# One weight DMA fewer and one zero product fewer in the tail of a decode kernel

## The chip, the core and the metric

The kernel runs on one core of one Trainium2 chip. The metric is the device time of one execution in microseconds (us). Each kernel was run several times; the medians are quoted together with the single runs where less than one per cent matters. All runs quoted here were classed "fast": none fell into the slower state that some executions show. A profile of one execution of each kernel gives the busy times, the waits and the timeline. Times inside a profile count from the start of its span, which is about 1.5 us shorter than the device time (660.1 against 661.56 us for the kernel before).

Engines are named as in the profile: PE is the engine of the matrix products, PEld its weight loads, DVE the vector engine, ACT the scalar engine, POOL the GpSimd engine, SP the sync engine, which issues nearly all DMAs here. A DMA "lands" when the last part of its data has come and its semaphore, for which the engines wait, has its full count.

## The reference, cut to what matters

One decode step of a transformer block for a batch of 4: attention over a cache of 4096 positions and 32 heads, then a dense layer with the Mish activation.

```python
x = A_x                                                    # (4, 1, 640), bf16
h = x + _A_ref(_layernorm(x), k_cache, v_cache, wq, wo)    # caches (4, 32, 4096, 128)
h2 = h + _B_ref(_layernorm(h), w1, b1, w2)                 # w1 (640, 1728), w2 (1728, 640)
# _A_ref: q = x @ wq; softmax(q k^T / sqrt(128)) v; then @ wo, wo (4096, 640)
# _B_ref: act = mish(x @ w1 + b1); act @ w2
```

Nearly all of the work is moving data: the two caches alone are 268 MB of the 283 MB that the kernel reads.

## The kernel before

SP issues the loads in the order of use: K and V tiles, then `wo`, `w1`, the last 64 rows of `w2` (`w2_tail`), and `w2` in four pieces of 5, 4, 3 and 1 row blocks. `wo` comes in four groups; the last group is cut into pieces of 4, 3 and 1 of its 8 rows per partition, so that PE can start on the first rows before the last have come.

```python
FR = (5, 4, 3, 1)                                   # w2's pieces, in blocks of 128 rows
FS = [sum(FR[:k]) for k in range(len(FR) + 1)]      # 0, 5, 9, 12, 13
WOS = [(k, 0, G) for k in range(NHG - 1)] + [(NHG - 1, a, b) for a, b in ((0, 4), (4, 7), (7, G))]
...
# SP
for n, (q, j0, j1) in enumerate(WOS):
    load(sp, wo_sb[:, q, j0:j1, :], A_wo[...][:, j0:j1, :], ("wo", q, j0), f"W{n}")
# then w1 in three pieces, w2_tail, w2 in the four pieces of FR; each has its own semaphore
```

On PE the tail is: products with `wo`; the layer norm's sums; products with `w1` into `h1`; then DVE and ACT compute Mish; then products with `w2`. Between them stand "zero products", which multiply zeros into a bank of PSUM (the memory that PE writes to) that nobody reads. They keep PE active while it waits.

```python
def busy(n):                                        # n products of 128 x 512 zeros
    for k in range(n):
        (mm_same if k else mm)(
            o_full[:, :], ident[:, :], zeros[:, :].to_broadcast([P, 512]), True, True
        )
...
pe.need("act")
def w2_mm(j): ...                                   # two products of 128 x 320, for the halves of the output
pe.need("w2t")
w2_mm(FM)
for j0, j1 in zip(FS, FS[1:]):
    if j0 == FS[2]:
        busy(3)                                     # ahead of w2's third piece
    pe.need(("w2", j0))                             # wait for this piece's DMA
    for j in range(j0, j1):
        w2_mm(j)
```

After the last product DVE and ACT copy the two halves of the output (`o_bf`), and SP and ACT store them.

The softmax here doesn't subtract the row's maximum and nothing guards it: scores larger than these inputs give would overflow.

Of the kernel before, what the change touches and what calls it, by code (L numbers as in the profile page):

```python
# [78 lines left out]
def kernel(  # L79
# [20 lines left out]
    G = 8  # L100
# [5 lines left out]
    NHG = H // G  # L106
# [135 lines left out]
    x_rows = A_x.rearrange("b s d -> (b s) d")  # L242
    out_rows = out.rearrange("b s d -> (b s) d")

    WOS = [(k, 0, G) for k in range(NHG - 1)] + [(NHG - 1, a, b) for a, b in ((0, 4), (4, 7), (7, G))]
    W1S = (0, 2, DC - 1, DC)

    KS = {0: "A", 1: "B", 2: "A", 3: "B"}
# [12 lines left out]
    def load(p, dst, src, key, sem):  # L261
        p.do(lambda: p.eng.dma_start(out=dst, in_=src), key, sem, 16)  # L262
# [43 lines left out]
    def sync_prog():  # L306
# [19 lines left out]
        sp.need(("F", NT - 1, NS - 1))  # L326
        for n, (q, j0, j1) in enumerate(WOS):
            load(
# [5 lines left out]
        for k, (c0, c1) in enumerate(zip(W1S, W1S[1:])):  # L334
            load(sp, w1_sb[:, c0:c1, :], w1_v[:, c0:c1, :], ("w1", c0), f"W{len(WOS) + k}")
        load(sp, w2_tail[0:FT, :], B_w2[FM * P : F, :], "w2t", "WT")
        sp.need(("PV", NT - 2))
        for k, (j0, j1) in enumerate(zip(FS, FS[1:])):
            load(
                sp, w2_sb[:, j0:j1, :],  # L340
                B_w2[j0 * P : j1 * P, :].rearrange("(p j) n -> p j n", j=j1 - j0), ("w2", j0),
                f"W{len(WOS) + len(W1S) - 1 + k}",
            )
# [376 lines left out]
    def mm(out_, lhsT, rhs, start, stop, mark=None, skip=True):  # L720
        pe.do(
            lambda: nc.tensor.matmul(  # L722
                out_, lhsT=lhsT, rhs=rhs, start=start, stop=stop, skip_group_check=skip
            ),
            mark, "PE",
        )
# [18 lines left out]
    def runs(cols, j):  # L745
        k, i = FG[j]
        cols = cols[:, FS[k] * P : FS[k + 1] * P].rearrange("p (f i) -> p i f", i=FR[k])
        return cols[:, i, :]
# [71 lines left out]
    def o_mm(i):  # L820
        b = i % N
        pe.need(("pvc", i))
        for r in range(RQ):
            mm(
                o_ps, selo[:, r, BG - G - b * G : 2 * BG - G - b * G], pv_sb[:, r, :],
                b == 0 and r == 0, b == N - 1 and r == RQ - 1, ("O", i) if r == RQ - 1 else None,
            )

    def l_mm(hg):
        pe.need(("rsm", hg))  # L830
        mm(l_ps, rsm[:, :, :].rearrange("p b g -> p (b g)"), ones[:, :], True, True, ("L", hg))

    def a_mm(hg):
        pe.need(("om", hg))
        w = om[:, :, :].rearrange("p g (q j) -> p j (g q)", j=G)
        for j in range(G):
            mm(
                a_ps[:, j, :], w[:, j, :], delta[:, :], True, True,
                ("A", hg) if j == G - 1 else None,
            )  # L840
# [25 lines left out]
    def pe_tail():  # L866
        def wo_mm(k):
            pe.need(("a", k))
            for j in range(G):
                if (k, j) in [w[:2] for w in WOS]:  # L870
                    pe.need(("wo", k, j))
                for c in range(DC):
                    w = wo_sb[:, k, j, :].rearrange("p (m c) -> p c m", c=DC)[:, c, :]
                    done = k == NHG - 1 and j == G - 1 and c == DC - 1
                    mm(
                        y_w[:, c, :, :], w, a_t[:, k, j, :].unsqueeze(1).to_broadcast([P, WD, N]),
                        False, done, "y" if done else None,
                    )

        def busy(n):  # L880
# [5 lines that stand above are left out]
        hg = NHG - 1  # L886
        pe.freeze()
        wo_mm(0)
        o_mm(NT - 1)
        l_mm(hg)  # L890
        wo_mm(1)
        a_mm(hg)
        pe.need("zeros", ("e", NT - 1, NS - 1))
        for k, w in enumerate((OC, OC, 512, 512)):
            (mm_same if k else mm)(
                red[:, k, 0:w], ident[:, :], zeros[:, :].to_broadcast([P, w]), True, False
            )
        wo_mm(2)
        wo_mm(3)
        busy(1)  # L900
        pe.need("ysum")
        mm(m_ps, ones_d[:, :], ysum[:, :], True, True, "mean")
        pe.need("sq")
        mm(sq_ps, ones_d[:, :], sq[:, :, :].rearrange("p c n -> p (c n)"), True, True, "sqm")
        busy(3)
        pe.need("cen")
        for c0, c1 in zip(W1S, W1S[1:]):
            if c1 == DC:
                pe.need("b1_lo")
                for n, part in enumerate((b1_hi, b1_lo)):  # L910
                    for j0, j1 in ((0, FC // 2 + 1), (FC // 2 + 1, FC)):
                        (mm_same if n or j0 else mm)(
                            h1_ps[:, j0:j1, :], ident[:, :], part[:, j0:j1, :], False, False
                        )
            pe.need(("w1", c0))
            for j in [FM] + list(range(FM)):
                for c in range(c0, c1):
                    w = runs(w1_sb[:, c, :], j) if j < FM else w1_sb[:, c, FM * P : F]
                    done = c == DC - 1 and j == FM - 1
                    mm(  # L920
                        h1_w[0 : (P if j < FM else FT), j, :, :], w,
                        cen[:, c, :].unsqueeze(1).to_broadcast([P, WD, N]), False, done,
                        "h1_ps" if done else None,
                    )
        pe.need("st", "ident_f")
        for c in range(DC):
            for k in range(KO):
                mm(
                    y2_ps[k * QD : k * QD + N, k, :].rearrange("b (m c) -> b c m", c=DC)[:, c, :],
                    st[:, c, :], ident_f[:, k * P // KO : (k + 1) * P // KO], False, False,  # L930
                )
        busy(4)
        pe.need("act")

        def w2_mm(j):
            rows = P if j < FM else FT
            for k in range(KO):
                cs = slice(k * OC, (k + 1) * OC)
                mm(
                    y2_ps[k * QD : k * QD + N, k, :], act[0:rows, j, :],  # L940
                    w2_sb[:, j, cs] if j < FM else w2_tail[0:FT, cs], False, j == FM - 1,
                    ("y2", k) if j == FM - 1 else None,
                )

        pe.need("w2t")
        w2_mm(FM)
        for j0, j1 in zip(FS, FS[1:]):
            if j0 == FS[2]:
                busy(3)
            pe.need(("w2", j0))  # L950
            for j in range(j0, j1):
                w2_mm(j)

    def pe_prog(live):
        pe.live = live
        pe_setup()
        pe.need("selo", "xT", "b1T")
        logs = []
        for hg in range(NHG):
            pe.log = []  # L960
            if live and hg == 0:
                with nc.tensor.Fori(0, NHG) as _:
                    pe_body(0)
                pe.live = False
            else:
                pe_body(hg)
            logs.append(pe.log)
        assert all(x == logs[0] for x in logs), logs
        pe.live = live
        pe_tail()  # L970
# [59 lines left out]
```

## Time and profile before

| | before |
|---|---|
| time, six runs | 661.54, 661.55, 661.62, 661.85, 661.87, 661.99 us; median 661.74 (the prediction had three of them, median 661.62) |
| profiled span | 660.1 us |
| mean rate of DMA over the span | 429 GB/s |
| `w1`'s second piece has landed | 651.13 us |
| `act` is computed | 655.05 us |
| `w2`'s third piece, its last row have landed | 657.2, 657.6 us |
| output copy on DVE starts | 658.21 us |

These six runs lie on two levels, about 661.6 and 661.9.

The page shows what bounds the kernel. These are the granted clock of PE, the busy share of the DMA engines (in tenths) and the rate, in 40 equal slices of the span.

```profile
PEclk9999787879659796869668678977965879786869
DMA  9999999999999999999999999999999999999997
GB/s 417 409 445 445 438 441 417 422 445 438 434 437 425 429 445 433 437 437 425 429 445 433 437 437 425 429 445 433 433 445 425 425 445 433 433 445 425 413 419 308
```

The DMA engines are full in all slices but the last. Only the last few microseconds can be a matter of anything else. The end of the chain of waits (start, length, what; it follows the last instruction back to what released it) reads:

```profile
651.13 0.04 issue
651.18 1.28 PE red L722 x29
...
654.83 0.23 DVE act L711
655.05 0.04 issue
655.10 1.68 PE red L722 x20
656.78 0.32 PE o_ps L722
657.10 0.43 PE o_ps L732 x2
657.54 0.69 PE red L722 x8
658.22 0.47 DVE o_bf L718
```

The `o_ps` entries are the zero products. They stand on the chain itself, which is odd for work that has no result. The timeline of PE, its weight loads and the copy shows how (start, length, engine, line, operation, what is written and read, count; in brackets the idle time of the engine before it, and what the profile believes ended it):

```profile
656.07 0.36 PEld L722 LDWEIGHTS red<-slotA,act 128*4 128x4 bf16 x8 [0.25 <-DMA slotA<-in_B_w_dram]
656.71 0.10 PEld L722 LDWEIGHTS o_ps<-zeros,ident 128*128 128x128 bf16 x1 [0.28 <-issue]
656.71 0.39 PE L722 MATMUL o_ps<-zeros,ident 128*128 128x512 bf16 x1
656.94 0.60 PE L732 MATMUL o_ps<-zeros,ident 128*128 128x512 bf16 x2
657.47 0.36 PEld L722 LDWEIGHTS red<-slotA,act 128*4 128x4 bf16 x8 [0.66 <-DMA slotA<-in_B_w_dram]
657.47 0.71 PE L722 MATMUL red<-slotA,act 128*4 128x320 bf16 x8
658.21 0.48 DVE L718 CAST o_bf<-red 4x320 bf16<-4x320 f32 x1 [3.17 <-PE red L722]
```

The line at 657.47 is the third piece (six loads) together with the last row (two). The bracket blames a DMA. To test that, take the issue of the two DMAs from the timeline of SP, and their time to landing from the DMA view:

```profile
640.92 1.25 SPq L262 DMA_DIRECT2D slotA<-in_B_w_dram  x1
642.21 0.97 SPq L262 DMA_DIRECT2D slotA<-in_B_w_dram  x1
...
slotA<-in_B_w_dram SPq DMA_DIRECT2D x1, 480.0 KB, 16.3
slotA<-in_B_w_dram SPq DMA_DIRECT2D x1, 160.0 KB, 15.4
```

The third piece landed at 640.92 + 16.3 = 657.2 us, the last row at 642.21 + 15.4 = 657.6 us. The semaphore events in the trace give 657.18 and 657.57 us. So the third piece lay there for 0.29 us before its first weights were loaded. What held it was the third zero product, which started at 657.16. The second piece, at 656.07, did wait for its data: it started 0.04 us after its landing (656.03).

### The profile page before, as it was taken

The page shows a single profiled execution, that of the slowest core. Times are in us where ns is not written, and L with a number is a line of the kernel's source. Part 1 is how long each engine was busy: PE and PEld are TensorE (multiplying, and loading weights), DVE is VectorE, ACT ScalarE, POOL GpSimd, SP SyncE. Part 2 cuts the span into 40 slices and gives each one's busy share as a digit, 9 for nine tenths or more (in the row PEclk, how much of TensorE's full clock was granted, in tenths as well). Part 3 has the DMA queues.
Part 4 walks back from the last instruction along what each step waited for, and adds up shares of the span by engine and source line. Part 5 has one row for each costly group of instructions (what it writes and reads, how often), then busy time and mean ns, then how long its engine had stood idle before and what let it go on. Part 6 is the DMA issues. An engine that isn't in the chain of part 4 may idle for free. (4 is left out here: it accounts for less than half of the span.)

```text
span 660.1 us, 4898 instructions
## 1 busy us (share of the span) xinstructions
PE 391.0 (59%) x2604; PEld 68.8 (10%) x1631; DVE 407.8 (62%) x255; ACT 41.1 (6%) x158; POOL 1.8 (0%) x13
## 2 busy tenths in 40 slices
PE   1365758456327595838307485828534757675878
PEld 0100100101101010101100010100110001010145
DVE  1078988295048778677219688848306798867612
ACT  0200000000000000000000000000000000000011
POOL 0000000000000000000000000000000000000000
PEclk9999787879659796869668678977965879786869
DMA  9999999999999999999999999999999999999997
GB/s 417 409 445 445 438 441 417 422 445 438 434 437 425 429 445 433 437 437 425 429 445 433 437 437 425 429 445 433 433 445 425 425 445 433 433 445 425 413 419 308
DMA packets 6883, 283.48 MB, mean 429 GB/s; under 512 B 781, under 2 KB 1113, under 8 KB 2138
## 3 DMA queue, kind: packets, MB, share of 16 engines
q1 hardware_dynamic: 6856, 283.35, 99.4%
q8 instruction: 6, 0.10, 0.1%
q14 instruction: 3, 0.02, 0.0%
q10 hardware_dynamic: 18, 0.01, 0.0%
HBM read 283.35 MB, written 0.01 MB: 429 GB/s over the span
## 5 line engine op out<-in xcount | busy, mean ns | idle before, releaser
L529 DVE TENSOR_TENSOR slotA<-slotA,q_bc 128x8192 bf16<-128x8192 bf16 x32 | 140.6, 4415 | 90.5 <-DMA slotA<-in_A_k_cache_dram 90.5
L529 DVE TENSOR_TENSOR slotB<-slotB,q_bc 128x8192 bf16<-128x8192 bf16 x32 | 140.7, 4416 | 16.5 <-DMA slotB<-in_A_k_cache_dram 16.5
L540 DVE TENSOR_REDUCE s_f<-red 128x64 f32<-128x1024 f32 x64 | 78.0, 1218 | 98.5 <-PE red L732 98.4
L732 PE MATMUL red<-slotA,ident 128*128 128x512 bf16 x480 | 137.5, 450 | 0.0
L732 PE MATMUL red<-slotB,ident 128*128 128x512 bf16 x480 | 127.3, 425 | 0.0
L722 PE MATMUL red<-slotA,ident 128*128 128x512 bf16 x32 | 14.2, 445 | 126.4 <-PEq L49 126.4
L722 PE MATMUL pv<-slotC,e 128*32 128x512 bf16 x768 | 53.1, 437 | 36.8 <-PEq L49 33.9
L722 PE MATMUL red<-slotB,ident 128*128 128x512 bf16 x32 | 14.1, 441 | 87.2 <-PEq L49 87.2
L402 ACT ACTIVATE ex<-s_f 128x64 bf16<-128x64 f32 x64 | 16.4, 256 | 512.0 <-DVE s_f L540 512.0
L554 DVE TENSOR_TENSOR e<-ex,hmask 128x512 bf16<-128x512 bf16 x64 | 39.8, 682 | 0.0
L722 PEld LDWEIGHTS pv<-slotC,e 128*32 128x32 bf16 x768 | 22.6, 108 | 95.7 <-issue 82.1
L722 PEld LDWEIGHTS red<-slotA,ident 128*128 128x128 bf16 x32 | 3.2, 99 | 195.1 <-issue 195.0
L722 PEld LDWEIGHTS red<-slotB,ident 128*128 128x128 bf16 x32 | 3.1, 98 | 169.2 <-issue 169.2
L722 PEld LDWEIGHTS o_ps<-pv_sb,selo 128*32 128x32 f32 x136 | 13.5, 109 | 65.1 <-issue 65.1
L722 PE MATMUL o_ps<-pv_sb,selo 128*32 128x128 f32 x136 | 18.0, 276 | 0.0
L722 PE MATMUL pv<-slotA,e 128*32 128x512 bf16 x256 | 14.5, 380 | 0.2 <-PEq L49 0.2
L412 ACT COPY pv_sb<-pv 128x512 f32<-128x512 f32 x16 | 9.4, 585 | 69.8 <-PE pv L722 69.8
L402 ACT ACTIVATION_READ_ACCUMULATOR ex<-s_f 128x1 f32 x64 | 11.9, 186 | 0.0
L722 PEld LDWEIGHTS pv<-slotA,e 128*32 128x32 bf16 x256 | 6.7, 97 | 23.4 <-issue 17.5
L519 DVE CAST b1T<-pv 128x13 bf16<-128x13 f32 x1 | 0.2, 173 | 14.0 <-PE pv L722 14.0
L579 DVE RECIPROCAL rl<-misc 32x1 f32<-32x1 f32 x4 | 0.6, 150 | 12.8 <-PE misc L722 12.8
L722 PE MATMUL red<-slotC,lnT 128*32 128x512 bf16 x40 | 4.5, 631 | 5.6 <-PEq L49 5.6
(105 smaller groups left out, 76.3 us busy)
## 6 DMA issues: line engine op xcount, KB each, us to landing
slotC<-in_A_v_cache_dram SPq DMA_DIRECT2D x2, 4096.0 KB, 39.0
slotC<-in_A_wq_dram SPq DMA_DIRECT2D x1, 5120.0 KB, 15.5
slotB<-in_A_wo_dram SPq DMA_DIRECT2D x3, 1280.0 KB, 15.6
slotB<-in_B_w_dram SPq DMA_DIRECT2D x2, 864.0 KB, 22.5
slotA<-in_B_w_dram SPq DMA_DIRECT2D x1, 800.0 KB, 18.5
slotB<-in_A_wo_dram SPq DMA_DIRECT2D x1, 640.0 KB, 19.3
slotA<-in_B_w_dram SPq DMA_DIRECT2D x1, 640.0 KB, 18.9
slotB<-in_A_wo_dram SPq DMA_DIRECT2D x1, 480.0 KB, 20.0
```

Source lines behind the costliest of these rows:

```text
L402: lambda: a.activation(out=ex[:, sl], in_=s_f[:, sl], func=ACT.Exp, scale=SCALE, accum_out=rs[:, b, s : s + 1],),
L412: lambda: a.copy(out=pv_sb[:, :, :].rearrange("p r d -> p (r d)"), in_=pv[:, :]),
L519: dv.do(lambda: v.tensor_copy(out=b1T[:, 0:FM], in_=b1_ps[:, 0:FM]), "b1m", DV)
L529: lambda: v.tensor_tensor(out=t, in0=t, in1=q_bc[:, hg, b, :].unsqueeze(1).to_broadcast([P, RS, Dh]), op=ALU.mult,),
L540: lambda: v.tensor_reduce(out=s_f[:, s * RS : (s + 1) * RS], in_=red[:, k : k + 2, :].rearrange("p k (r c) -> p (k r) c", c=CW), axis=AX.X ...
L554: lambda: v.tensor_tensor(out=e[:, sl, :], in0=ex[:, sl].unsqueeze(2).to_broadcast([P, RS, G]), in1=hmask[:, :].unsqueeze(1).to_broadcast( ...
L579: dv.do(lambda: v.reciprocal(out=rl[:, :], in_=l_ps), ("rl", hg), DV)
L722: lambda: nc.tensor.matmul(out_, lhsT=lhsT, rhs=rhs, start=start, stop=stop, skip_group_check=skip),
L732: return t.add_instruction(mybir.InstMatmult(name=nc.get_next_instruction_name(), engine=mybir.EngineType.PE, ins=[t.lower_ap(rhs), t.lowe ...
```

## The change

The last group of `wo` comes in two DMAs, of 5 and 3 rows, in place of three. That takes one DMA and 128 packets off the stream. With the data a little earlier, fewer zero products should fill the time ahead of `w2`'s third piece: two in place of three.

```diff
-    WOS = [(k, 0, G) for k in range(NHG - 1)] + [(NHG - 1, a, b) for a, b in ((0, 4), (4, 7), (7, G))]
+    WOS = [(k, 0, G) for k in range(NHG - 1)] + [(NHG - 1, a, b) for a, b in ((0, 5), (5, G))]
...
             if j0 == FS[2]:
-                busy(3)
+                busy(2)
             pe.need(("w2", j0))
```

## The prediction

> **What bounds the kernel now.** The DMA stream. The page's slices show the 16 DMA engines at 90% or more in 39 of 40 slices, 429 GB/s over the 660.1 us span. Only the last few us are a dependency chain. The chain of waits ends with: w1's second piece lands (651.13 us), 42 products into h1, Mish on DVE and ACT, `act` at 655.05, w2's products, output copy at 658.22, store. Landing times are a DMA's issue (timeline of SP) plus its time to landing (DMA view): wo's last group 645.0, 646.2, 646.75; w1 648.7, 651.1, 652.4; w2's pieces 654.5, 656.03, 657.18, 657.57.
>
> Within w2 (timeline of PE and PEld, 655 to 658 us), PE has finished the first piece at 655.9 and idles until the second lands (first weight load at 656.07). The three zero products start at 656.71, 656.94 and 657.16. The third piece has landed at 657.18, but its first weight load starts only at 657.47: it waits about 0.29 us behind the third zero product, although the timeline names a DMA. The last row's weights load at 657.74, its products end at about 658.18; that row had landed at 657.57.
>
> **The change.**
> 1. wo's last group in two DMAs: one DMA less, 128 packets fewer (row sizes 5120, 3840, 1280 B become 6400, 3840 B), same bytes. Packet durations in the trace: 10240 B 385 ns, 5120 B 196, 3840 B 149, 1280 B 55: about 7 ns per packet besides the bytes. An engine has 8 packets per DMA, and one 4-byte packet of 9 ns that signals completion (the Trainium skill, "DMA: Bandwidth & Descriptors", section on why a DMA increments its semaphore by 16, says each engine ends with such a write; the trace agrees). Estimate: 8 x 7 + 9, about 0.065 us off the stream; w1 and w2 land that much earlier. One SP issue of 0.43 us goes, worth nothing: SP later sits blocked in its issues for up to 4.3 us.
> 2. Cost: rows 5 and 6 come only at about 646.7 instead of 646.2. PE reaches row 5 at about 646.65 (43 ns per product), so it may wait 0.1 us. That is off the path: h1's first piece ends 0.9 us before w1's second lands.
> 3. One zero product less: PE is free for the third piece at 657.25 - 0.065, just when the data is there (657.22 - 0.065). Then the last row is bound by its own landing: 657.57 + 0.04 - 0.065 = 657.55 in place of 657.74. Its products end 0.3 to 0.38 us later, 657.85 to 657.93, against 658.18.
> 4. Clock: granted 1.00 over the last 20 us; the skill's "TensorE: Matmul & The Clock Gate", part 1, puts the idle window that re-throttles at about 3.4 us; the new gap is under 0.2 us. No loss expected.
>
> **Predicted.** About 0.25 to 0.33 us of 661.62 saved, two thirds from the zero product: 661.33 us, range 661.08 to 661.70. Faster by over 2%: 0.003; within 2%: 0.994; slower: 0.003.
>
> **What would show it.** Right: w1 and w2 land 0.05 to 0.1 us earlier; the third piece's first load within 0.06 us of its landing; the last row's load about 0.04 us after its landing; wo's products gain a wait of at most 0.15 us. Wrong: landings unmoved or later, or a granted clock below 1 in the last 5 us.
>
> **What would make it wrong.** The DMA engines finish up to 2.4 us apart on one DMA; a shift of the slowest engine, or an instruction fetch of 16 KB falling on it, is bigger than my whole effect. Runs of the kernel before spread over 0.44 us.

## The result and the profile after

| | before | after |
|---|---|---|
| median of six runs | 661.74 us | 661.34 us |
| single runs | 661.54, 661.55, 661.62, 661.85, 661.87, 661.99 | 661.30, 661.33, 661.34, 661.34, 661.35, 661.82 |
| profiled span | 660.1 us | 659.9 us |

The ratio is 0.9995, with a 95% interval of 0.9982 to 1.0008. It is worked out by code from the runs and is not quite the ratio of the medians. By that interval alone the two are the same. But the lower level moved from about 661.57 (mean of the three lower runs of before) to 661.33 (mean of the five lower ones after), 0.24 us, and the medians' difference of 0.40 us contains, besides this, that three runs of six lay on the upper level before and one of six after.

The profiles agree with 0.24 us. The same lines of the timeline, after:

```profile
656.06 0.36 PEld L722 LDWEIGHTS red<-slotA,act 128*4 128x4 bf16 x8 [0.32 <-DMA slotA<-in_B_w_dram]
656.70 0.10 PEld L722 LDWEIGHTS o_ps<-zeros,ident 128*128 128x128 bf16 x1 [0.28 <-issue]
656.70 0.39 PE L722 MATMUL o_ps<-zeros,ident 128*128 128x512 bf16 x1
656.93 0.38 PE L732 MATMUL o_ps<-zeros,ident 128*128 128x512 bf16 x1
657.24 0.45 PEld L722 LDWEIGHTS red<-slotA,act 128*4 128x4 bf16 x8 [0.44 <-DMA slotA<-in_B_w_dram]
657.24 0.71 PE L722 MATMUL red<-slotA,act 128*4 128x320 bf16 x8
657.98 0.48 DVE L718 CAST o_bf<-red 4x320 bf16<-4x320 f32 x1 [3.02 <-PE red L722]
```

In these lines the two timelines are the same within 0.01 us up to the start of the second zero product. Then the third piece starts at 657.24 in place of 657.47, and the output copy at 657.98 in place of 658.21: 0.23 us, and the whole difference of the spans. The eight weight loads now last 0.45 us in place of 0.36, because the last two wait for their own data, as these lines of SP's timeline and of the DMA view show:

```profile
641.09 1.53 SPq L262 DMA_DIRECT2D slotA<-in_B_w_dram  x1
...
slotA<-in_B_w_dram SPq DMA_DIRECT2D x1, 160.0 KB, 16.5
```

The last row landed at 641.09 + 16.5 = 657.6 us, by the semaphore events at 657.56. That is where it had landed before, to 0.01 us. Its weights were loaded at 657.61. So the shorter DMA stream, the first reason for the change, is not to be seen at the stream's end in this pair of profiles, and the zero product accounts for everything there. The shorter stream may show earlier: `w1`'s second piece landed at 650.95 in place of 651.13, and `act` was computed 0.09 us earlier. That went into a longer wait for `w2`'s second piece, which landed at 656.02 as against 656.03.

### The profile page after: what moved, and what is told of

Its sections match the earlier page's. It is cut to its first block, busy times and chain, and to the rows that moved or that the text cites. A ratio compares the mean times of both kernels' runs of the same rounds, so it can differ in the third digit from the quotient of the medians. Undisturbed runs are those within 1.5% of the kernel's fastest.

```text
span 659.9 us, 4896 instructions
## 1 busy us (share of the span) xinstructions
PE 383.9 (58%) x2603; PEld 68.3 (10%) x1631; DVE 407.7 (62%) x255; ACT 41.1 (6%) x158; POOL 1.8 (0%) x13
## 5 line engine op out<-in xcount | busy, mean ns | idle before, releaser
L732 PE MATMUL red<-slotA,ident 128*128 128x512 bf16 x480 | 134.6, 443 | 0.0
L732 PE MATMUL red<-slotB,ident 128*128 128x512 bf16 x480 | 125.0, 419 | 0.0
L722 PE MATMUL red<-slotA,ident 128*128 128x512 bf16 x32 | 14.4, 451 | 128.0 <-PEq L49 128.0
L722 PE MATMUL red<-slotB,ident 128*128 128x512 bf16 x32 | 13.9, 435 | 89.7 <-PEq L49 89.7
```

The lines of the kernel that those rows point to most:

```text
L722: lambda: nc.tensor.matmul(out_, lhsT=lhsT, rhs=rhs, start=start, stop=stop, skip_group_check=skip),
L732: return t.add_instruction(mybir.InstMatmult(name=nc.get_next_instruction_name(), engine=mybir.EngineType.PE, ins=[t.lower_ap(rhs), t.lowe ...
```

## The experiments

Three theories were set against each other.

- **A**: the third zero product held data back that had already landed. Taking it out gives its step of 0.22 us, until the data's own landing binds. The saved DMA gives at most a few hundredths of a microsecond.
- **B**: the DMA stream ends earlier, and the zero product only follows it.
- **C**: a zero product costs 0.22 us wherever it stands, so each further one taken out gives as much again.

All kernels gave correct results. The runs of before beside each group of experiments had medians of 661.74, 661.67 and 661.71 us, on three chips.

### The zero product alone

```diff
-                busy(3)
+                busy(2)
```
(on the kernel before; `wo`'s last group stays in three DMAs)

> The kernel before with two zero products in place of three, and wo's last group still in three DMAs. Theory A (the gain is the third zero product, which holds w2's third piece back by 0.29 us after it has landed; the saved DMA reaches the end with at most 0.02 us): landings of w2 as before (last row at 657.57 +-0.03 us), third piece's first weight load at about 657.25, output copy on DVE at about 657.99 in place of 658.21, time 0.2 to 0.25 us under before, as the whole change. Theory B (the gain is a DMA stream that ends earlier; the zero product only follows it): the output copy stays within 0.08 us of before, and so does the time.

Measured: 661.37, 661.40, 661.46, 661.50 and 661.96 us, median 661.46 against 661.74 for before (ratio 0.9997, interval 0.9984 to 1.0011). The timeline:

```profile
656.94 0.38 PE L732 MATMUL o_ps<-zeros,ident 128*128 128x512 bf16 x1
657.25 0.45 PEld L722 LDWEIGHTS red<-slotA,act 128*4 128x4 bf16 x8 [0.44 <-DMA slotA<-in_B_w_dram]
...
658.00 0.48 DVE L718 CAST o_bf<-red 4x320 bf16<-4x320 f32 x1 [2.94 <-PE red L722]
```

The last row landed at 657.58. Third piece at 657.25, copy at 658.00, as theory A had them. In these single profiles the zero product alone brings 0.21 of the 0.23 us.

### The two DMAs alone

```diff
-... ((0, 4), (4, 7), (7, G))]
+... ((0, 5), (5, G))]
```
(the changed kernel with `busy(3)` put back)

> The changed kernel with three zero products put back, so that only the wo DMAs differ from before. Theory A: w2's last row lands within 0.03 us of 657.57, third piece's first load again at about 657.46, time within 0.08 us of before. Theory B: landings of w2 0.06 us or more earlier, and time 0.15 us or more under before. Both: wo's products get a wait of 0.2 to 0.35 us in front of row 5, which does not reach the end.

Measured: 661.53, 661.58, 661.74, 661.77 and 661.79 us, median 661.74, the same as before (ratio 0.9999, interval 0.9986 to 1.0013). The timeline:

```profile
646.73 0.68 PEld L722 LDWEIGHTS y_ps<-a_t,slotB 128*128 128x128 bf16 x15 [0.17 <-DMA slotB<-in_A_wo_dram]
...
656.96 0.60 PE L732 MATMUL o_ps<-zeros,ident 128*128 128x512 bf16 x2
657.49 0.36 PEld L722 LDWEIGHTS red<-slotA,act 128*4 128x4 bf16 x8 [0.66 <-DMA slotA<-in_B_w_dram]
...
658.23 0.48 DVE L718 CAST o_bf<-red 4x320 bf16<-4x320 f32 x1 [3.24 <-PE red L722]
```

The last row landed at 657.58, the copy started at 658.23, as in the kernel before. Theory B falls as the cause of this gain. The first line is the price of the larger piece: PE waits 0.17 us ahead of row 5 of `wo`'s last group (0.2 to 0.35 had been expected), and this doesn't reach the end: the products of `w1`'s first piece end at 650.35, and its second piece lands only at 651.06.

### One DMA, and eight

```diff
-... ((0, 5), (5, G))]
+... ((0, G),)]                                  # one DMA of 10240-byte rows
+... [(i, i + 1) for i in range(G)]]             # eight DMAs of 1280-byte rows
```
(two kernels, each from the changed one; the one with eight DMAs also gets more semaphores)

> The changed kernel with wo's last group in one DMA of 10240-byte rows. By packet arithmetic (7 ns a packet, 8 packets an engine, 9 ns for the signal) the stream is 0.065 us shorter again. Theory A: that is lost before w2 lands, the time is within 0.06 us of the changed kernel; all 40 products of the group wait for its landing at about 646.6, they end about 0.9 us later than in the changed kernel, h1's first products end at about 651.2, after w1's second piece (650.95), and this is absorbed by the wait for w1's third piece at about 652.35. Theory B: 0.06 us or more faster than the changed kernel.

> The changed kernel with wo's last group in eight DMAs of one row (1280-byte packets), six DMAs more than the changed kernel. By packet arithmetic the stream is 6 x 0.065 = 0.39 us longer. Theory B: wo's last row and all of w2 land 0.35 to 0.45 us later, and the time is 0.35 to 0.45 us over the changed kernel. Theory A (the stream gives back part of what a DMA costs before its end): wo's last row lands 0.2 to 0.4 us later, w2's last row by 0 to 0.2 us, and so the time.

Measured with one DMA: 661.37, 661.44, 661.44, 661.49 and 661.61 us, median 661.44. The last row landed at 657.52, 0.04 us earlier than in the changed kernel, but the output copy started at 658.09, 0.11 us later. The timeline:

```profile
654.99 0.22 DVE L711 SCALAR_TENSOR_TENSOR act<-tb,hm 128x56 bf16<-128x56 f32 x1
...
656.81 0.39 PE L722 MATMUL o_ps<-zeros,ident 128*128 128x512 bf16 x1
657.04 0.38 PE L732 MATMUL o_ps<-zeros,ident 128*128 128x512 bf16 x1
657.35 0.36 PEld L722 LDWEIGHTS red<-slotA,act 128*4 128x4 bf16 x8 [0.44 <-DMA slotA<-in_B_w_dram]
```

All products of `wo`'s last group now wait for one landing, at 646.68. They end 1.1 us later, at 648.57, `act` comes 0.25 us later (654.99 against 654.74), and PE runs through `w2`'s first two pieces without a wait. It reaches the zero products 0.11 us later than in the changed kernel, and they hold the third piece until 657.35, although it landed at 657.13. I had expected the delay to be absorbed by the wait for `w1`'s third piece. It was not, because the products for `w1`'s first two pieces then ran to 652.6, past that landing (652.31). The same two zero products that were harmless one run earlier are on the chain again.

Measured with eight: 661.62, 661.63, 661.68, 661.98 and 662.02 us, median 661.68. The last row landed at 657.81, 0.25 us later than in the changed kernel, and the copy started at 658.24, 0.26 us later. Theory B had 0.35 to 0.45 us, theory A at most 0.2, so neither was met: a DMA does reach the end of the stream, but with less than its packets' durations. The median is 0.06 us under before, that with one DMA 0.30. Six DMAs more cost 0.25 us at the end of the stream, 0.04 us each, not the 0.065 us of the prediction's arithmetic.

### The changed kernel again, and fewer or more zero products

> The changed kernel once more, to have it on the same chip and in the same rounds as the next three. Output copy on DVE at 657.98 +-0.03 us, last row of w2 landing at 657.56 +-0.03, most runs 0.2 to 0.25 us under most runs of before; if theory A is right and one wo DMA is worth 0.035 us, about 0.04 us under the kernel with the zero product taken out alone.

> The changed kernel with one zero product in place of two. Theory A (the gain ends where the data's own landing begins to bind): the third piece's first load comes at its landing + 0.04 = 657.22 us, 0.02 us earlier than with two; the last row's load stays at its landing + 0.04 = 657.60; output copy and time within 0.04 us of the changed kernel. Rival theory C (each zero product costs its 0.22 us wherever it stands): another 0.2 us faster.

> The changed kernel with six zero products in place of two. Theories A and C: the products hold the third piece back by 4 x 0.22 = 0.87 us: first load at 658.11 us, output copy at 658.85, time 0.85 to 0.9 us over the changed kernel. If the time rises by much less, zero products do not hold PE up and theory A falls.

The edits are `busy(1)` and `busy(6)` in place of `busy(2)`. Measured, on one chip, beside before with a median of 661.67:

| kernel | runs (us) | median | third piece lands, first load | copy on DVE |
|---|---|---|---|---|
| `busy(1)` | 661.28, 661.34, 661.37, 661.39, 661.53 | 661.37 | 657.21, 657.25 | 657.99 |
| `busy(2)`, the changed kernel | 661.26, 661.32, 661.38, 661.51, 661.76 | 661.38 | 657.61, 657.66 | 658.40 |
| `busy(6)` | 662.26, 662.32, 662.39, 662.42, 662.45 | 662.39 | 657.39, 658.33 | 659.08 |

With one zero product the third piece starts 0.04 us after its landing, so its own data binds. The time is that of the changed kernel to 0.01 us. Theory C, which had another 0.2 us, falls. Its last two lines of weight loads show the two waits, one behind each landing:

```profile
656.72 0.39 PE L722 MATMUL o_ps<-zeros,ident 128*128 128x512 bf16 x1
657.25 0.23 PEld L722 LDWEIGHTS red<-slotA,act 128*4 128x4 bf16 x6 [0.43 <-DMA slotA<-in_B_w_dram]
...
657.63 0.08 PEld L722 LDWEIGHTS red<-slotA,act 128*4 128x4 bf16 x2 [0.15 <-DMA slotA<-in_B_w_dram]
```

With six, the first load comes 1.41 us after the first zero product (656.92 to 658.33). With two it was 0.54 us (656.70 to 657.24 in the first profile). The difference, 0.87 us, is what had been expected of four more products at 0.22 us each. The median rose by 1.01 us, 0.14 us more than that. In the profiled run `w2`'s second piece landed 0.2 us later than usual (656.24 against 656.02). Whether this belongs to the kernel or to the run was not settled.

The profiled run of the changed kernel was, by chance, the slowest of its five (661.76), so its profile missed what had been expected of it. It shows what made this run slow: the waits are the same ones, but `w2`'s last row landed at 657.99 in place of 657.56, and the copy started 0.42 us later. The semaphore events show the landings of the 16 DMA engines one by one. The whole stream was 0.2 us later than in the first profile of this kernel (mean landing 656.89 against 656.70), and it was so already at the last half of V (633.47 against 633.23). On top of that, 15 engines had landed by 657.67, and one came 0.32 us after them; a DMA has landed when its slowest engine has. What made the stream and that engine late the trace doesn't show.

### One DMA and no zero product

```diff
-... ((0, 5), (5, G))]
+... ((0, G),)]
...
-            if j0 == FS[2]:
-                busy(2)
```

> A version that might beat both: wo's last group in one DMA and no zero product ahead of w2's third piece. The run with one DMA and two zero products had w2's last row at 657.52 us, but its third piece was held by the zero products until 657.35, 0.22 us after its landing at 657.13. Theory A: without them the third piece's first load comes at 657.17, the last row's at 657.56, output copy at 657.94, time 0.03 to 0.08 us under the changed kernel. Theory C: 0.4 us under it. If PE loses its clock without zero products, the products of w2 take longer than 0.067 us each and the time is above the changed kernel's.

Measured beside the three kernels of the last table: 661.21, 661.29, 661.30, 661.32 and 661.43 us, median 661.30. The timeline:

```profile
657.23 0.46 PEld L722 LDWEIGHTS red<-slotA,act 128*4 128x4 bf16 x8 [0.70 <-DMA slotA<-in_B_w_dram]
...
657.97 0.48 DVE L718 CAST o_bf<-red 4x320 bf16<-4x320 f32 x1 [2.77 <-PE red L722]
```

The third piece landed at 657.19 and starts at 657.23; the copy starts at 657.97, 0.12 us earlier than with one DMA and two zero products. Without zero products the clock stays at 1.00 from 655 to 658 us, and the eight products take 0.71 us as before. The median is 0.08 us under that of the changed kernel on this chip. That is the expected size, but the runs of the two overlap, so it is not shown to be faster.

### What a DMA costs at the end of a full stream

```diff
-WOS = [(k, 0, G) for k in range(NHG - 1)] + [(NHG - 1, a, b) for a, b in ((0, 5), (5, G))]
+WOS = [(k, i, i + 1) for k in range(NHG) for i in range(G)]   # wo in 32 DMAs of one row
```
(with more semaphores, as for eight DMAs)

> The changed kernel with all of wo in 32 DMAs of one row (1280-byte packets) in place of 5: 27 DMAs more. By the prediction's arithmetic from packet durations a DMA costs 0.065 us (8 x 7 + 9 ns), so w2's last row would land 1.75 us later (659.3) and the time be 1.75 us over the changed kernel. By the runs with one and eight DMAs a DMA costs 0.035 to 0.04 us at the end of the stream, so w2's last row would land 0.95 to 1.1 us later (658.5 to 658.65) and the time rise by the same. If the time rises by over 2.5 us, the issues of SP have become the limit and the run says nothing about a DMA's own cost.

> The changed kernel, for the same chip and rounds as the next run. Theory A: 0.2 to 0.3 us under before; within 0.06 us of the next run, of which 0.035 us would be the saved DMA.

> The kernel before with two zero products in place of three once more, beside the whole change on the same chip. Theory A: the median is 0 to 0.06 us over the whole change's, and 0.2 to 0.3 us under before. If it is over 0.12 us slower than the whole change, the DMAs carry a real part of the gain.

Measured, beside before with a median of 661.71:

| kernel | runs (us) | median | last row lands | copy on DVE |
|---|---|---|---|---|
| `wo` in 32 DMAs | 662.64, 662.68, 662.80, 663.84, 663.91 | 662.80 | 658.84 | 659.25 |
| the changed kernel | 661.25, 661.27, 661.35, 661.43, 661.74 | 661.35 | 657.48 | 657.92 |
| before with `busy(2)` | 661.36, 661.44, 661.47, 661.49, 661.86 | 661.47 | 657.58 | 658.01 |

With 32 DMAs the last row landed 1.36 us later and the copy started 1.33 us later than in the changed kernel. For 27 DMAs more that is 0.05 us each; the median rose by 1.45 us. Both expectations missed: 1.75 us by packet durations is too much, 0.95 to 1.1 us by the earlier runs too little. SP's issues were not the limit in the profiled run: the last piece of `wo` was issued at 642.19 and landed at 647.83, so SP was still 5.6 us ahead, and the DMA engines had no gap to fill (busy share 1.07 from 634 to 648 us; the section on the prediction says how it can exceed 1). Two of its five runs lie another 1.1 us higher; why was not looked into, and the profiled run was not one of them.

The landing of the slowest engine is a noisy measure. The mean over the 16 engines is better, counted from the mean landing of the last half of V, which comes ahead of `wo` in all kernels. From the semaphore events of all thirteen profiles:

```
wo's DMAs in all      w2's last row after V's last half (mean of 16 engines, us)
4  (last group in 1)  23.40, 23.37                               mean 23.385
5  (in 2)             23.47, 23.43, 23.43, 23.42, 23.51, 23.40   mean 23.443
6  (in 3)             23.45, 23.49, 23.49                        mean 23.477
11 (in 8)             23.67
32 (all in rows)      24.72
```

From 4 to 32 DMAs the stream grows by 1.33 us, 0.048 us a DMA; between 6 and 5 the difference is 0.03 us, no more than the single profiles scatter. So a DMA less ends the stream earlier by an estimated 0.03 to 0.05 us, which a single pair of profiles can't show. The two kernels with two zero products differ by 0.12 us in their medians here, over the 0 to 0.06 that had been expected and on the edge of what had been set as telling; between the earlier groups, each taken from its own before, the difference is 0.01 us (0.29 against 0.28 us under before). What the DMA adds to the gain is therefore not settled by the times, beyond "between nothing and 0.12 us"; by the landings it is about 0.03 us.

## Why the prediction was right, and where it was not

1. **The time.** Predicted 661.33 us (661.08 to 661.70), measured 661.34. The closeness is partly luck: before came out at 661.62 in its first three runs and at 661.74 in six. The range also holds 661.62 itself, the time before as the prediction knew it, so the time alone says little about the mechanism. The predicted gain of 0.25 to 0.33 us compares with 0.23 us in the profiles, 0.24 us between the lower levels of the runs, and 0.40, 0.29 and 0.36 us between the medians of the changed kernel and before in the three groups that have both. Taken each beside its own before, the eight results with two zero products or fewer and at most six DMAs for `wo` are 0.24 to 0.40 us faster by their medians, and the one with three zero products not at all. The forecast of "within 2%" was right.

2. **The zero product.** Right in mechanism and size. The prediction read from the landings that the bracketed "DMA" could not be what the third piece waited for, and that the third zero product was. The run with the zero product alone gave 0.21 us; the run with six gave 0.87 us for four more; the run with one gave nothing further, because the last row's own landing had become the bound, as step 3 of the prediction said (657.61 for its first load against 657.74 before; 657.55 had been predicted with the shift of the stream).

3. **The saved DMA.** The term of the sum that was mis-sized. The prediction put "about 0.065 us off the stream; w1 and w2 land that much earlier". In the first pair of profiles `w2`'s last row landed 0.01 us earlier; of `w1`'s three pieces only the second came clearly earlier, by 0.19 us. For `w2` that is the sign which the prediction itself had listed as "Wrong: landings unmoved". Over all profiles a DMA is worth 0.03 to 0.05 us. The failed step is adding up packet durations. In the runs with eight and with 32 DMAs the pieces of 160 KB landed 0.42 us apart, while eight packets of 55 ns and the signal of 9 ns add up to 0.449 us. The pieces of 1280 KB landed 3.05 us apart, where eight of 385 ns and the signal make 3.09. So durations overcount each DMA by about 0.03 us in both cases; 0.065 less 0.03 is 0.035 us. The trace shows why: packets overlap in it. These lines are of the run with 32 DMAs and of the changed kernel, while `wo` comes in:

```profile
core 0: us, PE busy (x) PEld busy (x) DVE busy (x) ACT busy (x) POOL busy (x), PEclk, DMA share, GB/s
634.00:648.00 14.00, 13.30 (x212) 10.00 (x210) 1.78 (x4) 1.87 (x2) 0.00 (x0) 0.81 1.07 396
634.00:648.00 14.00, 13.43 (x217) 10.03 (x214) 2.21 (x7) 1.87 (x2) 0.00 (x0) 0.86 1.01 425
```

   The DMA share is the sum of the packets' durations over the time of 16 engines. It can exceed 1 only where packets on one engine overlap, and 1.07 is also 0.449 over 0.42.

4. **The share.** "Two thirds from the zero product" is not settled. It was 0.21 of 0.23 us in the profiles and 0.28 against 0.29 us in the medians of the earlier groups, but 0.24 of 0.36 us, two thirds, in the medians of the last group.

5. **wo's products.** A wait "of at most 0.15 us" ahead of row 5 was predicted; the run with two DMAs alone shows 0.17 us (in the changed kernel's own trace the weight loads pause for 0.13 us there). It stays off the path, as predicted. The run with one DMA shows how near the path is: there the wait grew, `act` came 0.25 us later, and two zero products were in the way again.

6. **The clock.** No loss was predicted, and there was none: granted 1.00 in the last 8 us with three, two, one and no zero products. The Trainium skill, "TensorE: Matmul & The Clock Gate", part 1, gives an idle window of about 3.4 us; the longest gap made here, 0.36 us ahead of the third piece without zero products, is far below it, which agrees, but no run here tests the window itself. At this place the zero products were not needed for the clock in these runs.

7. **What might have made it wrong** was named rightly: in the profile of the slow run, the stream and one lagging DMA engine put the last landing 0.43 us back, more than the whole effect.

## What to carry to other kernels

Filler work ahead of a wait is harmless only while it ends before the data lands. Where the timeline puts such a wait down to a DMA, work out the landing from the issue and the time to landing, and compare it with the end of the work in front; what was tuned for one arrival falls onto the chain as soon as anything shifts. Don't add up packet durations to price a DMA: change the number of DMAs, a lot, and measure where the end of the stream goes.

## What the Trainium skill lacked or had wrong

- **What one more DMA costs in a stream that is full.** "DMA: Bandwidth & Descriptors", section on bandwidth (measured), gives 6.15 us and 341 GB/s for 1 MB, and a fixed cost of about 2 us in the anatomy of one DMA (both for the GpSimd path). It has no figure for what one DMA more costs among DMAs that SP queues one behind the other. Here one more DMA cost 0.03 to 0.05 us, and DMAs of 160 KB landed every 0.42 us (163,840 bytes in 0.42 us, 390 GB/s), those of 1280 KB every 3.05 us (430 GB/s).
- **The limit of HBM.** The specifications of the same page put the limit for one core at about 358 GB/s, and its section "Where 436 GB/s comes from" says that this side binds for loads; elsewhere it notes that a lone core gets near 425. This kernel, run on one core, read 429 GB/s over 660 us, above that limit.
- **Slow DMA engines.** The page's table of latency and other measured facts says that engines 7 and 15 are usually slower, and ties its best guess for the cause to the GpSimd path alone. It has no figure for how far apart the engines end a load from SP, as all of these are. In the kernel before the 16 engines landed `w2`'s last row from 655.80 to 657.57 us, in two crowds: eight up to 656.37, eight from 656.95. Which engines are the late ones the trace doesn't say.
- **From a zero product to the next weights.** No page that was read has it: a load of 4-column weights started 0.31 us after the start of the last product of 128 x 512 zeros, where the next such product would have started after 0.22 us.
